# First gate maxima of an mLSTM reach their rows by products with a selection matrix instead of a trip through DRAM

## The chip, the cores and the metric

The kernel runs on one core of a Trainium2 chip. The metric is the device time of one execution in microseconds (us); the median of three runs stands for a kernel. Traces come from one further, profiled execution, whose span runs from the first to the last instruction of the program.

## What is computed

An mLSTM over 4 sequences of 768 tokens (8 heads of 40), followed by two mixture blocks on its 3072 x 320 output. All inputs and outputs count as float32, the weights of the blocks are given as float64. Cut to what matters:

```python
m_new = np.maximum(f_gate[:, :, t] + m, i_gate[:, :, t])       # running maximum of the gates
f_stab, i_stab = np.exp(f_gate[:, :, t] + m - m_new), np.exp(i_gate[:, :, t] - m_new)
C = f_stab * C + i_stab * (v k^T);  n = f_stab * n + i_stab * k
y[:, :, t] = sigmoid(o_gate) * (C q) / max(|n q|, 1)
...
h = (x @ w1) * (x @ w2) @ w3;  x = h @ w_out                    # first block
h = max(x @ w1, x @ w2, x @ w3);  out = h @ w_out               # second block
```

## The kernel before, in words

**Chunks.** Each sequence is cut into 9 chunks of 87 tokens (the last has 72), so there are 36 chunks, number q = 9 b + c. In a chunk the recurrence becomes matrix products: scores k.q, weighted by a decay matrix dd = exp(a_s - g_t) for key s and query t, where g is the running maximum of the gates (less the summed forget gates) and a is the gate value of each key. `prepare` (L786) loads a chunk's q, k and v, `visit` (L821) issues its score products (L839) and the products with v (L848), and `decay` (L744) makes dd.

**The gates** (L533 to L618) come by one DMA to 96 partitions: partition 32 i + 8 b + h holds chunks 3 i to 3 i + 2 of head h in sequence b. DVE scans them (L574, L585); the ends of the chunks are gathered to 32 partitions, scanned over the chunks, and spread again (L595, L607). L612 then leaves the running maxima in the tile gft, still on 96 partitions.

**The first nine decays** (q < 9, the chunks of sequence 0) are made by TensorE. A product (L757) of hl[0] (128 rows x 127 keys for each chunk) with hl[1] (128 rows x 8 heads x 88 queries) gives a_s - g_t for four heads at once, a second product (L758) adds -1e30 above the diagonal, and ScalarE takes the exponential (L761). To keep float32 precision with TensorE's faster operand type, every operand is split into a high part and the rest. Rows 0 to 63 of hl[0] hold the two parts of a, with unit rows of heads against them in hl[1]; rows 64 to 72 and 96 to 104 of hl[1] hold the two parts of g for the nine chunks, with -1 against them in hl[0]. So the maxima of sequence 0 have to get from partition 32 i + h, columns (c, t), to row 64 + 3 i + c, columns (h, t). Before the change that is a trip through DRAM: three writes to d_na (L619), one read back to the tile rv (L650), a ScalarE copy that makes the high part (L651) and a DVE subtraction that makes the rest (L652). GpSimd clears rows 64 to 127 of hl[1] first (L623). The other sequences write their maxima to d_na as well (L679), and the later decays read them from there; this part stays.

**Exponentials and sigmoids.** Five sigmoids of the first output gates (L667), on a tile loaded by L664, are made in one go, and every exponential of a decay is ordered behind all five (`after=sig`), since sigmoid and exponential use different tables of ScalarE.

**The folds.** The first block's w3 and w_out are multiplied on the chip (`fold`, L1227), eight times 16 product instructions of 320 columns (L1236); the result goes to wb (L1255, L1259). The weights come in granules of 128 x 512 float64 over the tiles sx and stg (`granule`, L1154): a DMA (L1167), a ScalarE step (L1172), a step that is made on DVE (L1181) or ScalarE (L1178), and a DVE step that joins the two (L1189). After the folds TensorE works through the two blocks, with the remaining chunks between their steps.

**The fill.** L541 issues 16 and then 6 products of zeros that warm up TensorE; the 6 wait for the first granule of w_out.

**What sets the order.** All this is written into a planner (`Plan`). Each operation has an engine (P TensorE, V DVE, A ScalarE, G GpSimd, D the DMA queue of SP), an estimated duration and the tiles that it reads and writes. A list scheduler takes, on each engine, the ready operation with the lowest entry in `PRIO`; where two engines can do an operation, `PICK` names one. The order that comes out is fixed in the program: every engine, and SP's DMA queue, works in that order and waits where an operation isn't ready. `WARM` tells the planner until when TensorE is slow.

```python
dma(150, lambda: SP.dma_start(out=raw_v, in_=d_na[0, :, :, 0:L]), r=[("dna", 0)], w=[("rv", 0)])   # L650
```

Of the kernel before, what the change touches and what calls it, by code (L numbers as in the profile page):

```python
# [65 lines left out]
    "11100111101000000100000110110011111101101111000111010011000110011110110011001110001111001011111110110000110010"  # L66
    "00001011101000111101100110011001101110001010010110011101001010110010111001101100101001110001001000001011111011"
    "10100110000001001110000011011110000100011011010111000100110110100000010000000000100100101000010100111101100110"
    "01000100010000101100001100010011010100110011110001011100000110011001110010111000000"
)  # L70
PRIO = (
# [95 lines left out]
)  # L167
WARM = 11500
USTEPS = (
# [1297 lines left out]
```

## Time and profile before

| | |
|---|---|
| median of three runs | 662.11 us (662.08 to 662.46) |
| the profiled execution: all of it | 664.29 us |
| the profiled execution: span | 662.6 us |
| mean granted TensorE clock | 0.997 |
| TensorE products busy | 648.7 us |
| DVE / ScalarE / GpSimd busy | 343.7 / 296.1 / 216.2 us |
| DMA | 76.12 MB, 115 GB/s on average |

The profiled execution is 2.18 us longer than the median. PE is TensorE's products, PEld its weight loads (which overlap products), ACT ScalarE, POOL GpSimd, SPq the DMA queue of SP. "Granted clock" is the share of full speed that TensorE was given.

### The profile page before, as it was taken

The numbers are of one execution on the slowest core, as the hardware profiler recorded it, in microseconds if no ns is written. First come the engines' busy times: TensorE is split into PE (matmuls) and PEld (weight loads), VectorE is DVE, ScalarE is ACT, GpSimd is POOL, SyncE is SP. The second block draws the span as 40 slices with busy tenths as digits, with TensorE's granted clock in tenths as the row PEclk, the third lists the DMA queues.
The fourth block names the chain that finished last, engine by engine and source line by source line (L and its number), as shares of the span: only waits on it lengthen the run. The fifth ranks groups of instructions, "written<-read, shape, count | busy, mean of one in ns | idle before, by whom it ended". The sixth has DMA issues, their size and how long they took to land.

```text
span 662.6 us, 14153 instructions
## 1 busy us (share of the span) xinstructions
PE 648.7 (98%) x5903; PEld 574.8 (87%) x5903; DVE 343.7 (52%) x623; ACT 296.1 (45%) x578; POOL 216.2 (33%) x235
## 2 busy tenths in 40 slices
PE   6899999999999999999999999999999999999997
PEld 5676899899999999999999988788788888888897
DVE  5688998877943663554543445464632321322222
ACT  7867986676622363453432343553331122322031
POOL 4052454566413234343244433562300013010030
PEclk9899999999999999999999999999999999999999
DMA  8989973545421453423122343342000010000011
GB/s 288 384 324 368 317 221 125 195 155 171 138 86 56 129 165 124 128 87 95 58 75 85 108 145 119 109 149 65 1 1 1 0 41 1 0 1 0 1 41 40
DMA packets 25489, 76.12 MB, mean 115 GB/s; under 512 B 3145, under 2 KB 6217, under 8 KB 25426
## 3 DMA queue, kind: packets, MB, share of 16 engines
q1 hardware_dynamic: 25426, 75.23, 33.8%
q8 instruction: 46, 0.75, 0.5%
q14 instruction: 17, 0.14, 0.1%
HBM read 71.18 MB, written 4.03 MB: 114 GB/s over the span
## 4 chain that ended last, share of the span: by engine, by line
PE 89%; DMA 3%; DVE 3%; ACT 3%; issue 1%; SPq 0%; ACTq 0%; DVEq 0%
PE wk L970 14%; PE wk L971 13%; PE wk L972 13%; PE wk L973 7%; PE acs L1102 6%; PE wk L975 5%; PE wk L1236 4%; PE aq L848 3%; PE acs L1082 3%; PE acs L1084 3%; PE acs L1086 3%; PE aq L839 3%; PE ac L1102 3%; PE ac L1082 2%; PE ac L1086 2%; PE wk L985 2%
## 5 line engine op out<-in xcount | busy, mean ns | idle before, releaser
L1049 DVE TENSOR_TENSOR misc<-misc,wk 128x384 f32<-128x384 f32 (+2 forms) x87 | 51.3, 594 | 130.5 <-PE wk L975 96.7
L997 ACT CAST hp<-misc 128x384 fp32r<-128x384 f32 (+2 forms) x101 | 55.0, 547 | 141.0 <-DVE misc L1049 53.1
L1001 POOL TENSOR_TENSOR hp<-misc,hp 128x384 fp32r<-128x384 f32 (+1 forms) x40 | 46.2, 1155 | 118.2 <-ACT hp L997 109.0
L970 PE MATMUL wk<-xx,wch 128*128 128x384 f32 (+1 forms) x216 | 77.3, 358 | 0.4 <-DVE misc L1049 0.4
L971 PE MATMUL wk<-xx,wcl 128*128 128x384 f32 (+1 forms) x216 | 76.5, 354 | 0.0
L972 PE MATMUL wk<-xx,wch 128*128 128x384 f32 (+1 forms) x216 | 76.5, 354 | 0.0
L1019 DVE TENSOR_TENSOR misc<-misc,wk 128x384 f32<-128x384 f32 (+1 forms) x56 | 33.8, 607 | 77.7 <-ACT misc L1017 53.2
L970 PE MATMUL wk<-xx,wah 128*128 128x384 f32 (+1 forms) x192 | 69.7, 363 | 1.1 <-DVE misc L1019 0.8
L971 PE MATMUL wk<-xx,wal 128*128 128x384 f32 (+1 forms) x192 | 68.1, 354 | 0.0
L972 PE MATMUL wk<-xx,wah 128*128 128x384 f32 (+1 forms) x192 | 68.0, 354 | 0.0
L1017 ACT COPY misc<-wk 128x384 f32<-128x384 f32 (+1 forms) x56 | 29.3, 522 | 54.8 <-PE wk L975 27.5
L1102 PE MATMUL acs<-wd,hp 128*128 128x320 f32 x234 | 52.7, 310 | 0.1
L1001 POOL TENSOR_TENSOR xx<-misc,hp 128x512 fp32r<-128x512 f32 (+1 forms) x15 | 18.2, 1215 | 95.5 <-ACT hp L997 91.3
L1046 ACT COPY misc<-wk 128x384 f32<-128x384 f32 (+1 forms) x42 | 22.1, 526 | 60.7 <-PE wk L975 46.2
L970 PEld LDWEIGHTS wk<-xx,wch 128*128 128x128 f32 x216 | 40.6, 188 | 3.7 <-DVE misc L1049 0.7
L972 PEld LDWEIGHTS wk<-xx,wch 128*128 128x128 f32 x216 | 40.5, 188 | 3.0
L971 PEld LDWEIGHTS wk<-xx,wcl 128*128 128x128 f32 x216 | 40.6, 188 | 2.8
L1236 PE MATMUL wk<-wof,w 128*128 128x320 f32 x128 | 38.4, 452 | 3.8 <-DVE wof L1189 2.3
L1102 PEld LDWEIGHTS acs<-wd,hp 128*128 128x128 f32 x234 | 40.0, 188 | 1.4 <-ACT misc L1145 0.3
L970 PEld LDWEIGHTS wk<-xx,wah 128*128 128x128 f32 x192 | 36.1, 188 | 4.6 <-DVE misc L1019 1.1
L972 PEld LDWEIGHTS wk<-xx,wah 128*128 128x128 f32 x192 | 36.1, 188 | 2.7
L973 PE MATMUL wk<-xx,wcr 128*128 128x384 f32 (+1 forms) x108 | 38.2, 354 | 0.0
(206 smaller groups left out, 1525.6 us busy)
## 6 DMA issues: line engine op xcount, KB each, us to landing
kv<-in_kv SPq DMA_DIRECT2D x32, 672.0 KB, 4.3
raw<-in_qk SPq DMA_DIRECT2D x36, 348.0 KB, 4.0
dd<-d_na SPq DMA_DIRECT2D x24, 348.0 KB, 3.8
sx<-in_w3t SPq DMA_DIRECT2D x9, 512.0 KB, 6.5
stg<-in_wc SPq DMA_DIRECT2D x9, 512.0 KB, 3.6
out<-misc SPq DMA_DIRECT2D x24, 160.0 KB, 1.9
stg<-in_w3t SPq DMA_DIRECT2D x6, 512.0 KB, 8.6
sx<-in_wa SPq DMA_DIRECT2D x6, 512.0 KB, 8.4
```

The source lines that it names most:

```text
L970: PE.matmul(p, lhsT=h_[:, kt], rhs=xh[:, kt], start=kt == 0, stop=False)
L971: PE.matmul(p, lhsT=l_[:, kt], rhs=xh[:, kt], start=False, stop=False)
L972: PE.matmul(p, lhsT=h_[:, kt], rhs=xl[:, kt], start=False, stop=False)
L973: PE.matmul(p, lhsT=r_, rhs=xh[:, 2], start=False, stop=False)
L975: PE.matmul(p, lhsT=r_, rhs=xl[:, 2], start=False, stop=True)
L997: P.op("A", act(n), lambda sl=sl: A.copy(out=T("ph", key)[:, sl], in_=T(*src)[:, sl]), r=[src + part], w=[("ph", key) + part])
L1001: e.tensor_tensor(out=T("pl", key)[:, sl], in0=T(*src)[:, sl], in1=T("ph", key)[:, sl].bitcast(F32), op=ALU.subtract)
L1019: P.op("V", dve(n), lambda: V.tensor_tensor(out=T(*sa), in0=T(*sa), in1=T(*ps[1]), op=ALU.mult), r=[ps[1]], w=[sa])
L1049: P.op("V", dve(sl.stop - sl.start), lambda sl=sl: V.tensor_tensor(out=T(*sc)[:, sl], in0=T(*sc)[:, sl], in1=T(*ps)[:, sl], op=ALU.max), r ...
L1082: PE.matmul(a, lhsT=w[:, o:o + 128], rhs=h_, start=st, stop=False)
L1102: PE.matmul(T(f"ac{m}", (k, 1)), lhsT=src[:, m * 128:m * 128 + 128], rhs=w[:, o:o + DM], start=first_, stop=last_,)
L1236: PE.matmul(T(*ps), lhsT=T(*w3)[:, i * 128:i * 128 + 128], rhs=wof[:, gt * 320:gt * 320 + 320], start=gt == 0, stop=gt == 7,)
```

## The change

The three writes, the read and the two splitting steps behind them are gone. Instead ScalarE makes the high part of gft and DVE the rest, both on 96 partitions, in a new tile gh (it lies in hp, as does sel). GpSimd builds a selection matrix sel (96 x 908, zeros but for a 1 in column 104 + i + 108 p of row 32 i + p). For each of the 8 heads, 6 products (two parts, three chunks of a partition) with a window of 112 columns of sel as weights and 88 columns of gh as moving operand add up to a PSUM tile rp in which every row is in place: rows 64 + 4 c + i for the high part, 96 + 4 c + i for the rest. ScalarE copies rows 64 to 111 of rp to hl[1], half the heads at a time. GpSimd clears rows 96 to 127 of hl[1] only; the pattern of -1 in hl[0] follows the new rows. The second part of the fill waits for gate values in the place of the first granule, and is ordered ahead of the new products. The planner's estimate for the load of the output gates goes from 1700 to 2050, WARM from 11500 to 8000, and all of PRIO and PICK is new.

```diff
 PICK = (
-    "1110011110100000010000011011001111110110111100011101001100011001111011001100111000111100101111111011000011
...
+    "0111010000100011100001011010100010110001111000010101111111000111100010110111110101000110111110110011110001
...
 PRIO = (
-    124, 456, 180, 57, 15, 275, 188, 113, 62, 171, 725, 164, 105, 490, 354, 463, 153, 364, 281, 60, 125, 68, 247, 137,
...
+    46, 26, 359, 120, 369, 213, 136, 142, 66, 141, 9, 8, 244, 134, 148, 319, 70, 72, 54, 28, 57, 50, 122, 37, 7, 2,
...
-WARM = 11500
+WARM = 8000
...
-    made["rv", 0] = misc[:, o:o + 8 * L]
...
+    made["gh", 0], made["sel", 0] = (hp[0:96, o:o + n].bitcast(F32R) for o, n in ((0, 2 * 3 * LE), (2 * 3 * LE, 908)))
+    made["gh", 0] = made["gh", 0].rearrange("p (x c t) -> p x c t", x=2, t=LE)
+    over["ph"] = over["pl"] = [("gh", 0), ("sel", 0)]
...
-    for n, dep in ((16, ()), (6, (("wo", 0, 0),))):
+    for n, dep in ((16, ()), (6, (("g", "git"),))):
...
-        e = cs[:, L + 1:L + 1 + NCH]
+        e = cs[:, L + 1:L + 1 + NCH].rearrange("p (i c) -> p i c", c=3)
         for o in (64, 96):
-            pick(e, e, 1, -o, [[-1, NCH]], ALU.not_equal, -1.0)
+            pick(e, e, 1, -o, [[-1, 3], [-4, 3]], ALU.not_equal, -1.0)
...
+    def f():
+        sel = T("sel", 0)
+        G.memset(sel.bitcast(F32), 0.0)
+        G.memset(T("gh", 0)[:, :, :, L:LE].bitcast(F32), 0.0)
+        for i in range(3):
+            sl = sel[32 * i:32 * i + 32]
+            pick(sl, sl.bitcast(F32), -108, -104 - i, [[1, 908]], ALU.not_equal, 1.0)
+
+    P.op("G", 36, lambda: G.memset(T("hl", 1)[96:128].bitcast(F32), 0.0), w=[("hl", 1, 2), ("hl", 1, 3)])
+    P.op("G", 3300, f, w=[("sel", 0), ("gh", 0, 2)])
...
-    for i in range(3):
-        dma(100, lambda i=i: SP.dma_start(
-            out=d_na[0, 3 * i:3 * i + 3].rearrange("c h t -> h c t"), in_=c3(T("g", "gft"))[32 * i:32 * i + 8]
-        ), r=[("g", "gft")], w=[("dna", 0, i)])
-
-    P.op("G", 400, lambda: G.memset(T("hl", 1)[64:128].bitcast(F32), 0.0), w=[("hl", 1, 2), ("hl", 1, 3)])
+    P.op("A", act(SL), lambda: A.copy(out=T("gh", 0)[:, 0, :, 0:L], in_=c3(T("g", "gft"))), r=[("g", "gft")], w=[("gh", 0, 0)])
+    P.op("V", dve(SL), lambda: V.tensor_tensor(
+        out=T("gh", 0)[:, 1, :, 0:L], in0=c3(T("g", "gft")), in1=T("gh", 0)[:, 0, :, 0:L].bitcast(F32), op=ALU.subtract
+    ), r=[("g", "gft"), ("gh", 0, 0)], w=[("gh", 0, 1)], port=1)
+    warm(1)
+    new(("rp", 0), [128, 2, 512], F32, "aq")
+
+    def rp(h):
+        return T("rp", 0)[0:112, h // 4, h % 4 * LE:h % 4 * LE + LE]
+
+    for g in range(2):
+
+        def f(g=g):
+            for h in range(4 * g, 4 * g + 4):
+                for x in range(2):
+                    for c in range(3):
+                        a = 40 + 108 * h - 32 * x - 4 * c
+                        PE.matmul(rp(h), lhsT=T("sel", 0)[:, a:a + 112], rhs=T("gh", 0)[:, x, c],
+                                  start=(x, c) == (0, 0), stop=(x, c) == (1, 2))
+
+        P.op("P", 24 * mm(LE), f, cols=24 * LE, r=[("gh", 0), ("sel", 0)], w=[("rp", 0, g)])
...
-    hi, raw_v = T("hl", 1)[64:64 + NCH, :, 0:L], T("rv", 0)[64:64 + NCH].rearrange("p (a b) -> p a b", b=L)
-    dma(150, lambda: SP.dma_start(out=raw_v, in_=d_na[0, :, :, 0:L]), r=[("dna", 0)], w=[("rv", 0)])
-    P.op("A", act(8 * L), lambda: A.copy(out=hi, in_=raw_v), r=[("rv", 0)], w=[("hl", 1, 2)])
-    P.op("V", dve(8 * L), lambda: V.tensor_tensor(
-        out=T("hl", 1)[96:96 + NCH, :, 0:L], in0=raw_v, in1=hi.bitcast(F32), op=ALU.subtract
-    ), r=[("rv", 0), ("hl", 1, 2)], w=[("hl", 1, 3)])
+    for g in range(2):
+        P.op("A", act(4 * LE, True), lambda g=g: A.copy(
+            out=T("hl", 1)[64:112, 4 * g:4 * g + 4], in_=T("rp", 0)[64:112, g, 0:4 * LE].rearrange("p (h t) -> p h t", t=LE)
+        ), r=[("rp", 0, g)], w=[("hl", 1, 2 + g)])
...
-    dma(1700, lambda: SP.dma_start(out=sg0.rearrange("p c d -> p (c d)"), in_=og),
+    dma(2050, lambda: SP.dma_start(out=sg0.rearrange("p c d -> p (c d)"), in_=og),
...
-            warm(1)
```

## Rows read from the trace of the kernel before

**Rows 1.** The page: busy us, share of the span and instructions of each engine.

```profile
PE 648.7 (98%) x5903; PEld 574.8 (87%) x5903; DVE 343.7 (52%) x623; ACT 296.1 (45%) x578; POOL 216.2 (33%) x235
```

**Rows 2.** Stretches: PE, PEld, DVE, ACT, POOL busy; granted clock, DMA share, GB/s.

```profile
12.00:14.00 2.00, 1.70 (x8) 1.20 (x8) 1.97 (x4) 1.33 (x2) 1.90 (x3) 1.00 1.01 272
14.00:16.00 2.00, 0.98 (x4) 0.38 (x2) 0.51 (x2) 1.33 (x3) 0.67 (x1) 1.00 0.86 286
16.00:18.00 2.00, 0.75 (x2) 0.62 (x3) 1.95 (x4) 2.00 (x4) 0.00 (x0) 0.91 0.99 365
18.00:20.00 2.00, 2.00 (x5) 1.27 (x4) 1.34 (x4) 0.82 (x2) 0.00 (x0) 0.50 0.98 397
```

**Rows 3.** Timeline of PE, 9.6 to 22 us: start, length, work [idle before].

```profile
11.11 1.15 PE L659 MATMUL ac<-cs,misc 32*127 32x32 f32 x9 [1.29 <-ACT sx L1172]
12.56 2.42 PE L1236 MATMUL wk<-wof,w 128*128 128x320 f32 x8 [0.30 <-DVE w L1189]
17.25 4.92 PE L1236 MATMUL wk<-wof,w 128*128 128x320 f32 x11 [2.27 <-DVE wof L1189]
```

**Rows 4.** The chain that ended last, whole span: start, length, link.

```profile
17.25 4.12 PE wk L1236 x8
...
33.57 2.15 PE wk L1236 x8
```

**Rows 5.** Timelines of ACT, 20 to 30 us, and of PE, 26.9 to 28.8 us.

```profile
23.99 0.77 ACT L651 CAST hl<-misc 9x696 fp32r<-9x696 f32 x1
...
26.02 0.83 ACT L667 ACTIVATE sg<-sg 96x320 f32<-96x320 f32 x2
...
28.17 0.46 ACT L761 ACTIVATE dd<-wk 87x348 f32<-87x348 f32 x1
...
28.67 0.54 PE L1236 MATMUL wk<-wof,w 128*128 128x320 f32 x1 [1.05 <-ACT dd L761]
```

**Rows 6.** SP's queue: timeline, 8 to 30 us; waits (us in all, times, longest).

```profile
17.86 0.30 SPq L650 DMA_DIRECT2D misc<-d_na  x1
...
SPq L650 <- DMA d_na<-misc: 2.8, 2, 2.6
```

**Rows 7.** Timeline of DVE, 11 to 18 us: the maxima.

```profile
11.14 0.43 DVE L612 TENSOR_TENSOR misc<-misc,mp 96x261 f32<-96x261 f32 x1
```

**Rows 8.** Groups of PEld, 0 to 30 us; then PE's timeline around 26 us.

```profile
L659 PEld LDWEIGHTS ac<-cs,misc 32*127 32x127 f32 x9 | 1.1, 185 | 1.7 <-POOL mp L595 1.7
...
25.59 0.85 PE L839 MATMUL aq<-raw 40*87 40x87 f32 x16
...
26.97 0.33 PE L758 MATMUL wk<-one 87*128 87x352 f32 x1
27.14 0.32 PE L757 MATMUL wk<-hl,hl 128*128 128x352 f32 x1
```

**Rows 9.** PE's waits after 60 us; the chain between 54 and 68 us.

```profile
PE wk L757 <- ACT dd L761: 1.1, 1, 1.1
PE wk L970 <- DVE misc L1019: 0.8, 1, 0.8
...
PE wk L757 <- ACT misc L1017: 0.2, 1, 0.2
...
55.74 7.37 DMA stg<-in_wa
```

**Rows 10.** POOL: a group by form, and its timeline before 8 us.

```profile
L780 POOL TENSOR_SCALAR_AFFINE_SELECT dd<-dd 87x696 f32<-87x696 f32 x24 | 21.4, 890 | 27.4 <-ACT dd L777 27.3
...
7.62 0.32 POOL L579 MEMSET misc<- 96x261 f32 x1 [4.17 <-DVE misc L574]
```

**Rows 11.** Timelines of DVE and POOL between 32 and 37 us.

```profile
32.93 0.68 DVE L1189 SCALAR_TENSOR_TENSOR w<-sx 128x512 int32<-128x512 int32 x1
...
34.67 1.82 DVE L1189 SCALAR_TENSOR_TENSOR w<-sx 128x512 int32<-128x512 int32 x1 [0.38 <-ACT sx L1178]
...
34.29 1.66 POOL L806 TENSOR_TENSOR pk<-kv,dd 63x696 f32<-63x696 f32 x1
```

More of the change, by code (lines that the diff above doesn't have):

```diff
@@ L65 @@
 PICK = (
[L66 to L69, printed above, removed]
+    "01110100001000111000010110101000101100011110000101011111110001111000101101111101010001101111101100111100011000"
+    "10010101001010000100101101101110111111010100101001111000100101101101000100110010111100000100000011010011111111"
+    "11111110101101100100010011110010100101111001101110101101000101010101011100101011100111001101010110101001110000"
+    "00100000110110110010100000011100101100111100000001001001101011000111011001110000000"
 )
 PRIO = (
[95 rows of a table removed]
[94 rows of a table added]
 )
-WARM = 11500
+WARM = 8000
 USTEPS = (
@@ L524, in mlstm_moe_kernel @@
         o += n
-    made["rv", 0] = misc[:, o:o + 8 * L]
-    for tag, (x, y) in where.items():
-        if x < o + 8 * L and o < y:
-            over[tag].append(("rv", 0))
+    made["gh", 0], made["sel", 0] = (hp[0:96, o:o + n].bitcast(F32R) for o, n in ((0, 2 * 3 * LE), (2 * 3 * LE, 908)))
+    made["gh", 0] = made["gh", 0].rearrange("p (x c t) -> p x c t", x=2, t=LE)
+    over["ph"] = over["pl"] = [("gh", 0), ("sel", 0)]
     def c3(t):
```

187 rows, old and new, of the table PRIO are left out of this document.

## Prediction

> **What bounds the kernel now.** I began with the page's table of engines: TensorE is busy for 648.7 of the 662.6 us of the span, every other engine for little more than half of it [rows 1]. So a change pays only where it shortens one of the few stretches in which TensorE does nothing useful, and it costs time where it gives TensorE work that doesn't fit into such a stretch. The changed code lies in the first 28 us, so I read those next, in steps of 2 us: between 12 and 18 us TensorE's share falls, and from 18 to 20 us its granted clock is 0.50, which is the 1.2 GHz level; the DMA engines stay near 1.0 there, apart from 14 to 16 us [rows 2]. The timeline of TensorE names the holes: it is idle for 1.29 us before the transposes at 11.11, for 0.30 before the first half of fold 0 at 12.56, and for 2.27 before the second half at 17.25 [rows 3]. That last hole ends with w_out granules which DVE finishes late; the trip through DRAM has no part in it. The second half, 8 instructions, then takes 4.12 us at the low clock, where 8 such instructions later take 2.15 [rows 4]: 1.97 us are lost to the clock, after a stretch of little TensorE work.
>
> Where does the trip itself end? Its last copy into hl[1] runs at 23.99 (DVE's subtraction follows), and the five sigmoids of the first output gates run around it until 26.85. The code lets no exponential of a decay start before all five, and another table of ScalarE has to be loaded first. The first exponential runs at 28.17, and TensorE idles 1.05 us for it [rows 5]. So the trip is mostly hidden behind the sigmoids; only its copy, 0.77 us, stands in ScalarE's order ahead of them. On SP's queue the trip costs more: three writes, then the read back, issued at 17.86 after a wait of 2.6 us for a write to land [rows 6].
>
> **The change, part by part.** My sum is made against the profiled execution (664.29 us in all, span 662.6); the median of the three plain runs, 662.11, is 2.18 lower, and I carry the difference over to it.
>
> *The products.* 48 products enter TensorE, each with a load of 112 columns of weights over 96 partitions and 88 moving columns; they can start when both parts of the maxima stand, about 12.6 us (the maxima are ready at 11.57 [rows 7], then a ScalarE and a DVE step of some 0.43 us each). No row shows such a product. The nearest is the nine transposes: loads of 127 columns that follow each other every (1.1 - 0.19)/8 = 0.114 us [rows 8], which for 112 columns is 0.10 us, or 4.8 us for 48. The lower end is the score products, 16 in 0.85 us: 0.053 each, 2.5 us. The upper end is the decay products of 352 columns, one every 0.16 us [rows 8]: 7.8 us, in case a product of few columns is charged like a long one. I take 4.8, since the transposes are the row with loads of nearly this size.
>
> One page speaks against the change here. The Trainium skill, "TensorE: Matmul & The Clock Gate", Part 3, "The mechanism", says that a weight load overlaps a running product only if it goes to other row groups, and all 48 use the same rows. The transposes also share their rows, and their loads ran on beneath the products, one every 0.114 us with a product of its own in each, so the trace doesn't bear the rule out.
>
> *What the products cover.* At 12.6 us they fill the hole of 2.27 us, and with TensorE at work there the clock should stay at its high level (2.4 GHz), which gives back 1.97. Together -4.2, against +4.8: +0.6 us for fold 0's end. The new ranks put the product groups (entries 24 and 25 of the list, counted from 0: 7 and 2) ahead of all of fold 0, so what is queued behind them is fold 0, and behind that everything on TensorE. If the clock stays low nevertheless, add 2.0.
>
> *ScalarE and the wait at 28.67.* The copy of 0.77 us and DVE's subtraction behind it leave this stretch. Added are a ScalarE copy and a DVE subtraction of 96 x 261 near 12 us and two evacuations of 352 columns (0.46 each, like the exponentials [rows 5]) near 18 us; in 14 to 20 us both engines have gaps [rows 2], so these cost nothing unless fold 0's granules come to stand behind them, at most 1.8 us. Of the wait of 1.05 us I take off 0.6: the sigmoids, and the gate values they load, still stand ahead. Bounds 0 and -1.05.
>
> *SP's queue and the DMA.* Four issues go, and the wait of 2.6 us, behind which loads of w3 for the folds were queued [rows 6]. But the DMA engines were 0.86 busy in 14 to 16 us and 0.99 after [rows 2], so they lose 0.14 x 2 = 0.3 us at least; by bytes, the 272 and 286 GB/s of 12 to 16 us against 365 just after, they lose (2 x 365 - 272 - 286)/365 x 2 = 0.9 us. That helps where TensorE waits for a load. The one such chain runs through w1's granule at 55.74 to 63.11 us and ends with a wait of 1.1 us [rows 9]. I take -0.6; bounds 0 and -0.9.
>
> *GpSimd.* It gets two clears and three selections of 32 x 908. From the selection of 696 columns, 0.89 us, each is 1.16; from the clear of 261, 0.32, the large clear is 1.11: 4.6 us, and a little for the small one. Its gap before 7.62 us is 4.17 [rows 10], and the clear of hl[1] shrinks to half its partitions. I cost it at nothing, covered by that gap; if the cover is short, the mask for the scan comes late, and with it the products.
>
> *The rest.* The transposes and their evacuation stay. Tile rp shares its place with the fill products, which end before the idle time of 1.29 us [rows 3], and with the first scores, which come at 25.59 [rows 8]: nothing. The fill's second part now waits for gate values instead of a granule; were it 1.29 us later, it would still end before the transposes can start: nothing. hp, in which the new operands lie, is first written when the first MoE block splits its products, long after the folds began: nothing.
>
> *The order.* All ranks and choices change, so any wait may move. After 60 us TensorE waits six times, for 1.1 us (the one above) and for 0.8, 0.5, 0.4, 0.3 and 0.2 [rows 9]: 2.2 us beside the first. I take 0 and allow 1.5 either way.
>
> Sum: 4.8 - 4.2 - 0.6 - 0.6 = **-0.6 us**: span 662.0, that execution 663.7, median **661.5**.
>
> **The rivals.** (a) *The products are cheap* and fit the hole with room to spare: at 0.053 us they take 2.5, so fold 0's second half starts when its granules stand and the sum is 2.3 lower, -2.9: 659.2. For it: the score products with 87 columns run at that rate. Against it: those use half the rows each, two at a time; these use 96. (b) *The products are dear*: 0.163 us each, 7.8 in all. Fold 0 ends 3.0 later than in my sum, and no idle time of that size stands between it and the end: +2.4, so 664.5, slower. It decides from about 0.14 us a product on (6.7 us, the sum then +1.3). For it: no product in the trace with this operand type has fewer than 320 columns. Against it: a load of 112 columns is the longer half of such a pair in the transposes. (c) *Loads and products take turns*: 0.10 + 0.163 x 88/352 = 0.14 us each, 6.8 us, sum +1.4: 663.5. That is the page's rule above; the transposes speak against it. (d) *GpSimd holds DVE*: a DVE step of two SBUF operands that takes 0.68 us took 1.82 while GpSimd worked [rows 11], and the selections now run while DVE turns the first granules and scans the gates, ahead of the maxima. One selection's length of delay, 1.16, on the gates and granules: sum +0.6, 662.7. The Trainium skill, "SBUF — State Buffer", "Who interferes with whom", describes this as a port pair that one of the two engines holds for a whole instruction; the 1.82 us agree. (e) *It doesn't matter*: the trip was hidden and the hole is given to other work; this lies inside my forecast's own range.
>
> **How the numbers follow.** About 0.2%, 1.3 us, is what a measurement can tell from no change. Chances: forecast 0.40, (a) 0.32, (b) 0.17, (c) 0.04, (d) 0.07. With its 1.5 us for the order and the bounds of the small terms, the forecast itself spans 660.0 to 663.0; of its 0.40 I put 0.06 faster than 660.8, 0.30 within 1.3 us of 662.1 and 0.04 above 663.4, where the order costs more than I allow. (a) is faster; (b) slower; (c) lies near the edge and is counted as slower; of (d) 0.06 is same and 0.01 slower. So faster 0.38, same 0.36, slower 0.26. The range runs from (a) less part (0.9) of the order's allowance, 658.3, to (b), 664.6.
>
> **What would show it.** Right: the 48 products every 0.10 us from about 12.6 us, no idle time before fold 0's second half, a granted clock near 1.0 from 16 to 22 us, fold 0 ended by 22 us, the first exponential some 0.8 us sooner, no SP wait near 17 us. Wrong: products spaced 0.14 us or more, the clock at 0.5 after them, or DVE steps before 8 us stretched beyond 1 us. If all that is right and the time still moves by over 1.5 us, the order did it: then TensorE's waits after 60 us differ from the list in [rows 9].

## The result, and the profile after

The changed kernel takes 669.47 us (667.89 to 669.79, 4 runs), the kernel before 662.29 on the same chip (662.08 to 662.84, 4 runs): 1.0102 times as long, 95% interval 1.0085 to 1.0120. It is slower by 7.2 us, and lies 4.9 above the upper end of the range. Its profiled execution took 669.34, with a span of 667.6 (5.0 above the one before) and a mean granted clock of 0.989.

The page's table of engines, beside [rows 1], and two rows of its 40 slices:

```profile
PE 657.3 (98%) x5951; PEld 583.4 (87%) x5951; DVE 341.4 (51%) x644; ACT 295.0 (44%) x577; POOL 193.5 (29%) x222
...
PE   7999999999999999999999999999999999999998
...
PEclk8799999999999999999999999999999999999999
```

TensorE has 48 more instructions and 8.6 us more busy time. The clock is down in the first two slices (17 us each) alone, so the loss is to be looked for there. TensorE's timeline of the changed kernel from the start (start, length, work, idle before it), beside [rows 3]:

```profile
1.67 6.88 PE L539 MATMUL aq<-wb 128*128 128x512 f32 x22 [1.67 <-DVE wb L533]
10.86 1.15 PE L681 MATMUL ac<-cs,misc 32*127 32x32 f32 x9 [2.32 <-DVE mp L604]
12.41 9.25 PE L644 MATMUL aq<-hp 96*112 96x88 f32 x48 [0.40 <-ACT hp L627]
21.45 4.42 PE L1257 MATMUL wk<-wof,w 128*128 128x320 f32 x8
25.40 0.63 PE L779 MATMUL wk<-hl,hl 128*128 128x352 f32 x1
25.87 0.33 PE L780 MATMUL wk<-one 87*128 87x352 f32 x1
26.03 2.32 PE L1257 MATMUL wk<-wof,w 128*128 128x320 f32 x8
```

From the first of the 48 products to the first of fold 0 (L1257) pass 21.45 - 12.41 = 9.04 us: 0.188 for each product, where I had 0.10. The holes ahead of fold 0's halves are gone, but fold 0 ends at 28.35 instead of 21.37. The stretches of the same execution, with the columns of [rows 2]:

```profile
10.00:12.00 2.00, 1.14 (x9) 1.07 (x9) 1.79 (x7) 1.20 (x2) 1.12 (x4) 0.97 1.03 418
12.00:14.00 2.00, 1.60 (x10) 1.61 (x9) 1.97 (x3) 1.95 (x4) 1.19 (x2) 0.50 1.04 423
14.00:16.00 2.00, 2.00 (x13) 2.00 (x13) 1.99 (x5) 0.00 (x0) 0.00 (x0) 0.50 0.99 397
16.00:18.00 2.00, 2.00 (x13) 2.00 (x12) 0.88 (x2) 0.00 (x0) 0.00 (x0) 0.50 1.01 321
...
24.00:26.00 2.00, 2.00 (x6) 1.33 (x6) 1.52 (x4) 1.97 (x3) 0.00 (x0) 0.62 0.03 8
26.00:28.00 2.00, 2.00 (x10) 1.36 (x8) 0.65 (x1) 1.31 (x3) 0.00 (x0) 1.00 0.83 264
```

The granted clock falls to 0.50 (1.2 GHz) just ahead of the first product, at about 11.9 us if the 0.97 of 10 to 12 us is one drop, and comes back only at about 25.5 (0.62 of 24 to 26), at the end of fold 0's first half. Weight loads (the second number) fill the whole of the stretches from 14 to 18 us. Two more things stand out: ScalarE has nothing to do between 14 and 20 us, and between 24 and 26 us the DMA engines rest. ScalarE's timeline (beside [rows 5]) and SP's queue (beside [rows 6]) say why:

```profile
21.75 0.45 ACT L674 CAST hl<-aq 48x352 fp32r<-48x352 f32 x1 [7.80 <-PE aq L644]
22.21 0.67 ACT L1194 ACTIVATE sx<-sx 128x512 f32<-128x512 f32 x1
...
31.78 0.46 ACT L783 ACTIVATE dd<-wk 87x348 f32<-87x348 f32 x1
```

```profile
17.79 7.90 SPq L1189 DMA_DIRECT2D stg<-in_w3t  x2
```

ScalarE's copy out of rp waits 7.80 us for the products, with granule steps (L1194) queued behind it, and SP's queue takes 7.90 us over two loads, 7.4 of them a wait for a DVE step (L1203) behind those. Which of these two, TensorE's own time or this blockade, makes the loss, the trace alone doesn't tell; the experiments do.

GpSimd's timeline, DVE's with a step that needs its mask, and the first two of TensorE's waits after 60 us, beside [rows 10] and [rows 9] (the DVE rows begin with the first scan of the gates):

```profile
2.82 2.91 POOL L546 TENSOR_SCALAR_AFFINE_SELECT hp<-hp 32x908 fp32r<-32x908 f32 x3
...
7.86 0.32 POOL L588 MEMSET misc<- 96x261 f32 x1
```

```profile
5.77 0.70 DVE L583 TENSOR_TENSOR_SCAN misc<-misc 96x261 f32<-96x261 f32 x1 [3.75 <-DMA misc<-in_gi]
...
8.37 0.70 DVE L594 TENSOR_TENSOR_SCAN misc<-misc 96x261 f32<-96x261 f32 x1 [0.83 <-POOL misc L589]
...
11.06 0.43 DVE L621 TENSOR_TENSOR misc<-misc,mp 96x261 f32<-96x261 f32 x1
```

```profile
PE wk L992 <- ACT misc L1068: 0.8, 1, 0.8
PE wk L992 <- DVE misc L1071: 0.6, 1, 0.6
```

The three selections took 2.91, the maxima stand at 11.49 (11.57 before), and the 1.1 us wait for an exponential isn't in the list any more.

### The profile page after: what moved, and what is told of

Same layout as the page of the kernel before. It is cut to its first block, busy times and chain, and to the rows that moved or that the text cites. A ratio compares the mean times of both kernels' runs of the same rounds, so it can differ in the third digit from the quotient of the medians.

```text
span 667.6 us, 14270 instructions
## 1 busy us (share of the span) xinstructions
PE 657.3 (98%) x5951; PEld 583.4 (87%) x5951; DVE 341.4 (51%) x644; ACT 295.0 (44%) x577; POOL 193.5 (29%) x222
## 4 chain that ended last, share of the span: by engine, by line
PE 88%; ACT 3%; DVE 3%; DMA 2%; issue 1%; POOL 1%; POOLq 0%; DVEq 0%; ACTq 0%
PE wk L992 13%; PE wk L993 13%; PE wk L994 13%; PE wk L995 6%; PE acs L1124 6%; PE wk L1257 5%; PE wk L997 5%; PE aq L870 3%; PE aq L861 3%; PE acs L1104 3%; PE ac L1124 3%; PE acs L1106 3%; PE acs L1108 3%; PE wk L1007 1%; PE wk L946 1%
## 5 line engine op out<-in xcount | busy, mean ns | idle before, releaser
L1023 POOL TENSOR_TENSOR hp<-misc,hp 128x384 fp32r<-128x384 f32 (+1 forms) x44 | 52.0, 1182 | 127.5 <-ACT hp L1019 116.5
L1257 PE MATMUL wk<-wof,w 128*128 128x320 f32 x128 | 38.9, 454 | 0.0
L895 DVE TENSOR_TENSOR pk<-aq,dd 87x696 f32<-87x696 f32 (+1 forms) x33 | 28.4, 862 | 19.3 <-PE aq L870 18.4
```

Source lines behind the costliest of these rows:

```text
L1023: e.tensor_tensor(out=T("pl", key)[:, sl], in0=T(*src)[:, sl], in1=T("ph", key)[:, sl].bitcast(F32), op=ALU.subtract)
L1257: PE.matmul(T(*ps), lhsT=T(*w3)[:, i * 128:i * 128 + 128], rhs=wof[:, gt * 320:gt * 320 + 320], start=gt == 0, stop=gt == 7,)
```

## The experiments

The theory (A): the products are paced by their weight loads, 112 columns each, and the load's pace follows the granted clock; the clock falls around 12 us, the products neither hold nor raise it, and so 48 of them take 9 us instead of 4.8. Its rivals: a fixed price for each product, or loads and products in turns (B); the blockade of ScalarE and SP's queue (D); the new order of everything else (C). "Before" is 663.05 us (661.01 to 665.39, 14 runs) beside the first four kernels, 663.04 (660.32 to 664.94, 23 runs) beside the next four, and 662.44 (660.11 to 666.2, 17 runs) beside the last three.

### e1_narrow: only the 48 columns that are read

Rows 0 to 63 of rp are zeros that nobody reads. Here the window of sel is 48 columns wide, and the result lies in rows 0 to 47.

```diff
-        return T("rp", 0)[0:112, h // 4, h % 4 * LE:h % 4 * LE + LE]
+        return T("rp", 0)[0:48, h // 4, h % 4 * LE:h % 4 * LE + LE]
...
-                        PE.matmul(rp(h), lhsT=T("sel", 0)[:, a:a + 112], rhs=T("gh", 0)[:, x, c],
+                        PE.matmul(rp(h), lhsT=T("sel", 0)[:, a + 64:a + 112], rhs=T("gh", 0)[:, x, c],
...
-            out=T("hl", 1)[64:112, 4 * g:4 * g + 4], in_=T("rp", 0)[64:112, g, 0:4 * LE].rearrange("p (h t) -> p h t", t=LE)
+            out=T("hl", 1)[64:112, 4 * g:4 * g + 4], in_=T("rp", 0)[0:48, g, 0:4 * LE].rearrange("p (h t) -> p h t", t=LE)
```

> Edit of the changed kernel: the products load 48 columns of sel (those of the rows that are used) in place of 112, and rp holds the rows at 0 to 47; what is computed and the order stay the same. Theory A (the products are paced by their weight loads, 0.187 us for 112 columns at the granted clock of 0.50): a product every 48/112 x 0.187 = 0.080 us, or 3.9 us for 48 where they took 9.25, so ScalarE, which waited 7.80 us for them, goes on 5.4 us sooner; the time falls by 3 to 5.4 us from 669.5, to 664.1 to 666.5. Rival B (a product of 88 columns costs 0.187 us whatever it loads): the pace and the 9.25 us stay, 669.5. Rival C (the new order later in the program costs the time, the products don't): the products may be faster, but the time stays within 1 us of 669.5.

Measured: 662.62 us (660.29 to 664.03, 10 runs), ratio to before 0.9992 (0.9973 to 1.0010). TensorE's timeline, then two of its stretches:

```profile
13.06 3.83 PE L644 MATMUL aq<-hp 96*48 96x88 f32 x45 [0.18 <-DVE hp L628]
16.68 3.60 PE L1257 MATMUL wk<-wof,w 128*128 128x320 f32 x8
...
20.45 2.32 PE L1257 MATMUL wk<-wof,w 128*128 128x320 f32 x8
```

```profile
14.00:16.00 2.00, 2.00 (x29) 2.00 (x28) 1.99 (x5) 0.02 (x1) 0.00 (x0) 0.50 0.98 393
...
18.00:20.00 2.00, 2.00 (x8) 1.37 (x6) 1.15 (x3) 1.93 (x5) 0.00 (x0) 0.72 0.86 262
```

45 products take 16.68 - 13.06 = 3.62 us, 0.080 each, at a clock of 0.50. The moving columns, the rows and the count are those of the changed kernel, and 0.188/0.080 = 2.35 is the ratio of the loads' columns, 112/48 = 2.33. So the 88 moving columns add nothing beside a load of 112. The whole loss goes with it, more than I had expected, since the clock is also back by 20 us instead of 26. B and C fall.

### e2_longfill: the clock held up to the products

```diff
-        def f(n=n):
+        def f(n=n + 8 * (n == 6)):
```

Eight more products of zeros in the fill's second part.

> Edit of the changed kernel: the second part of the fill has 14 products of zeros where it had 6, so that TensorE has dense work to about 10.3 us, where it fell idle at 8.5; the order stays the same. Theory A1 (the clock fell at 11.9 us because TensorE was idle from 8.5 to 10.9, and products then run at the clock they find): granted clock 1.0 from 12 to 26 us, the products every 0.094 to 0.10 us, 4.7 us in all, fold 0's products at 0.27 us each; the time falls by 5.5 to 7, to 662.5 to 664. Theory A2 (the products with their short moving side can't keep the clock up): the clock falls a few us later than 11.9, within the products or behind them, the time falls by 1 to 4. Rival B (the cost of a product doesn't come from the clock): products at 0.187 us, time 669.5 or more.

Measured: 668.22 us (667.09 to 670.05, 5 runs), ratio 1.0068 (1.0043 to 1.0092). The transposes ahead of the products:

```profile
11.10 1.15 PE L681 MATMUL ac<-cs,misc 32*127 32x32 f32 x9 [0.61 <-DVE mp L604]
```

The products' line in two stretches, 13.3 to 15.3 us and 16 to 19 us (form, count: shortest/median/longest in ns, first and last start), and the clock from 14 us on:

```profile
L644 PEld LDWEIGHTS aq<-hp x22: 173/178/178, 13.3 to 15.3; 96*112 96x112 f32 x22
...
L644 PEld LDWEIGHTS aq<-hp x18: 307/307/307, 15.8 to 18.9; 96*112 96x112 f32 x18
```

```profile
14.00:16.00 2.00, 2.00 (x21) 2.00 (x21) 1.99 (x4) 0.21 (x1) 0.00 (x0) 0.91 0.99 399
16.00:18.00 2.00, 2.00 (x13) 2.00 (x12) 1.12 (x3) 0.00 (x0) 0.00 (x0) 0.50 0.84 293
```

One kernel, one stream of products, both prices: at the high clock 22 loads start within 2.0 us, 0.10 apart, which is the value I had taken; then the clock falls in the middle of the products, though TensorE never pauses, and 18 loads need 3.1 us, 0.18 apart. So here the products did not hold the clock, as theory A2 has it. The estimate of a product was right for 2.4 GHz; the assumption of 2.4 GHz was not.

### e3_zeros_between: more work among the products

```diff
                                   start=(x, c) == (0, 0), stop=(x, c) == (1, 2))
+                PE.matmul(acs[:, 512 * x:512 * x + 512], lhsT=wb[:, NA - 1, 512:640], rhs=wb[:, NA - 1, 0:512], start=True, stop=True)
```

After each six products, one of 512 columns of zeros.

> Edit of the changed kernel: one product of zeros with 512 columns behind each six of the new products, eight in all, into a PSUM tile that is not yet in use; nothing else. Work added: 8 x 0.43 = 3.4 us at the low clock, 8 x 0.22 = 1.8 at the high one. Theory A (the low clock is what the products cost): either the denser work lifts the clock within the products, then they and the fold behind them run at the high clock sooner and the time falls by 1 to 4 us in spite of the work added; or it doesn't, then the clock stays at 0.50 to 26 us or later, and the time rises by up to 3.4, to 673. Rival B: the clock may rise, but the products stay at 0.187 us and the time rises by 1.8 or more.

Measured: 672.13 us (671.64 to 675.04, 4 runs), ratio 1.0137 (1.0097 to 1.0177). Two of its stretches:

```profile
20.00:22.00 2.00, 2.00 (x10) 1.88 (x10) 0.00 (x0) 0.00 (x0) 0.00 (x0) 0.50 1.00 387
...
26.00:28.00 2.00, 2.00 (x5) 1.22 (x4) 1.06 (x3) 1.93 (x5) 0.00 (x0) 0.50 0.00 0
```

The clock stayed at 0.50 until 28 us, and the median is 2.7 us above the 669.47 of the changed kernel, within the 3.4 allowed. More work of this kind between the products didn't lift the clock here. Since the clock never rose, this run doesn't tell A from B; e1 and e2 do.

### e4_before_again: the kernel before, profiled once more

> The kernel before, once more, for its granted clock: the profiled execution shown had a stretch at 0.50 from 17.4 to 21.4 us and took 664.29 us, the plain runs 662.1. If that stretch comes and goes from execution to execution, a profile without it spans about 660.5 us and takes 662.2; if it belongs to the kernel, it is there again, at the same place, with 664.3 us.

Measured: 660.28 us, one execution, mean clock 1.000. Its timeline around fold 0, and the stretch that had a clock of 0.50 in [rows 2]:

```profile
12.04 2.42 PE L1236 MATMUL wk<-wof,w 128*128 128x320 f32 x8 [0.30 <-DVE w L1189]
15.39 6.73 PE L1236 MATMUL wk<-wof,w 128*128 128x320 f32 x24 [0.93 <-DVE wof L1189]
```

```profile
18.00:20.00 2.00, 2.00 (x9) 1.44 (x8) 1.38 (x4) 1.98 (x3) 0.00 (x0) 1.00 1.03 403
```

Here the kernel before has no stretch at the low clock, and its hole is 0.93 us, not 2.27. So much of the 4.2 us that the products were to cover wasn't there in this execution. Of the 54 executions of the kernel before beside the experiments 16 have a mean clock of 0.999 or 1.000, so the low stretch is short or missing in those too; how long their holes were is not on record.

### e5_narrow_longfill: both together

The edits of e1_narrow and e2_longfill in one kernel.

> Edit of the changed kernel: both edits of before, 48 columns of weights and 14 products of zeros in the second part of the fill. The clock held to 15.6 us with the longer fill, and a product with 112 columns then came every 0.0985 us. Theory A (a product is paced by its load): 48/112 x 0.0985 = 0.042 us each, 2.0 in all, where the narrow products alone took 3.8 at the low clock. A1: with the products over by 15 us the clock doesn't fall, fold 0 runs at 0.27 us a product: 3.5 us less than the 662.6 of the narrow products alone, 659. A2: it falls behind the products all the same, and fold 0 runs at half the rate: 1.8 less, 660.8. Rival B (a floor of some 0.08 us for each product, whatever its load): 662.

Measured: 662.10 us (660.05 to 666.88, 12 runs), ratio 0.9991 (0.9973 to 1.0009): no gain over e1_narrow that can be told. That is the number of rival B, a floor of 0.08 for each product; the trace doesn't decide it, for its clock was low during most of the products, but e11 does (below). The profiled execution, the slowest of the twelve, has this stretch:

```profile
12.00:14.00 2.00, 1.28 (x15) 1.10 (x15) 1.97 (x3) 2.00 (x5) 1.27 (x2) 0.75 1.04 424
```

Here the clock fell at the beginning of the products, in spite of the longer fill. In five of the twelve executions the mean clock was 1.000, in none of the 22 of e1 and e9 over 0.997; but those five took 660.05 to 663.84 too. So the longer fill carries the clock through at times, and with narrow products that is then worth little.

### e6_copies_dont_wait: the blockade without its cause

```diff
-            out=T("hl", 1)[64:112, 4 * g:4 * g + 4], in_=T("rp", 0)[64:112, g, 0:4 * LE].rearrange("p (h t) -> p h t", t=LE)
+            out=T("hl", 1)[64:112, 4 * g:4 * g + 4], in_=wb[0:48, NA - 2, 0:4 * LE].bitcast(F32).rearrange("p (h t) -> p h t", t=LE)
```

ScalarE's two copies read a constant, in a tile that DVE sets early, so the kernel leaves out that the maxima reach the decays; the 48 products still run.

> Edit of the changed kernel: the two copies into hl[1] read a tile with a constant (set early by DVE), not rp. This leaves out that the maxima reach the decays; the 48 products of 112 columns still run, but nothing reads them. Theory A (TensorE's own time is what counts): ScalarE no longer waits 7.80 us, the granules are turned sooner, but the products still take 9.25 us at the low clock and fold 0 starts at 21.5 us: the time falls by less than 1.5 from that of the changed kernel beside it. Rival D (ScalarE, blocked behind the products, starves the folds and SP's queue, and that is the greater part): the time falls by 3 or more.

Measured: 669.65 us (669.51 to 670.99, 4 runs), ratio 1.0105 (1.0079 to 1.0131), beside 668.88 for the changed kernel in the same group (e8). TensorE, and one stretch:

```profile
12.31 9.25 PE L644 MATMUL aq<-hp 96*112 96x88 f32 x48 [0.22 <-ACT hp L627]
21.35 4.32 PE L1257 MATMUL wk<-wof,w 128*128 128x320 f32 x8
```

```profile
24.00:26.00 2.00, 2.00 (x7) 1.37 (x6) 0.00 (x0) 0.00 (x0) 0.00 (x0) 0.69 1.02 389
```

The DMA engines are busy between 24 and 26 us now (1.02 instead of 0.03), and ScalarE has nothing left to do in that stretch; the time doesn't fall. D falls: the blockade, the most striking thing in the trace, cost nothing here.

### e7_no_products: the rest of the change alone

```diff
-                        PE.matmul(rp(h), lhsT=T("sel", 0)[:, a:a + 112], rhs=T("gh", 0)[:, x, c],
-                                  start=(x, c) == (0, 0), stop=(x, c) == (1, 2))
+                        pass
```

and the copies as in e6.

> Edit of the changed kernel: as the one whose copies read a constant, and the 48 products left out, so that the maxima don't reach the decays; order and all else stay the same. Theory A (the products are the loss): fold 0 starts near 12.5 us and the time falls by 8 to 10.5 from that of the changed kernel beside it, to 659 to 661.5, below the kernel before. Rival C (the new order and the other new steps cost time too): it stays above 663.

Measured: 663.78 us (663.09 to 664.63, 10 runs), ratio 1.0013 (0.9997 to 1.0029). TensorE's timeline:

```profile
15.13 4.55 PE L1257 MATMUL wk<-wof,w 128*128 128x320 f32 x8 [3.29 <-DVE w L1211]
...
19.84 2.32 PE L1257 MATMUL wk<-wof,w 128*128 128x320 f32 x8
```

The products cost 669.65 - 663.78 = 5.9 us against e6, from which this kernel differs by them alone (5.1 against e8); the rest of the change, order and all, 0.7 against the kernel before, which this run can't tell from nothing. I had expected more to come back, and by the bound that I gave (above 663) the run went rival C's way, though it lies level with the kernel before. The reason is that without the products fold 0 waits 3.29 us for a granule that DVE joins at 14.65 (behind its subtraction for hl[0]), and then starts at the low clock: the products do cover a hole, and the new order has made it longer than the 2.27 and 0.30 of [rows 3] together.

### e8_changed_again: the changed kernel beside e5 to e7

> The changed kernel once more, on the chip of the other runs of this group, as their base. 669.5 within 1 us; granted clock 0.50 from about 12 to 26 us again, products every 0.187 us. If its clock falls later in this execution, the products before the fall come every 0.0985 us, as in the run with the longer fill.

Measured: 668.88 us (668.47 to 670.06, 4 runs), ratio 1.0092 (1.0066 to 1.0118). The 45 products behind the first three took 8.42 us, 0.187 each, as before. The clock fell somewhat later here, among the first products (0.70 on average from 12 to 14 us).

### e9 to e11: can the rest be won by order?

e9 is e1_narrow again. e10 gives DVE's subtraction for hl[0] a later rank, so that fold 0's granule is joined first; e11 also ranks the second 24 products behind fold 0's first half.

```diff
-    206, 1, 33, 124, 103, 153, 196, 239, 117, 52, 203, 335, 41, 186, 536, 74, 422, 283, 464, 738, 133, 349, 221, 334,
+    206, 1, 33, 900, 103, 153, 196, 239, 117, 52, 203, 335, 41, 186, 536, 74, 422, 283, 464, 738, 133, 349, 221, 334,
```

```diff
-    46, 26, 359, 120, 369, 213, 136, 142, 66, 141, 9, 8, 244, 134, 148, 319, 70, 72, 54, 28, 57, 50, 122, 37, 7, 2,
+    46, 26, 359, 120, 369, 213, 136, 142, 66, 141, 9, 8, 244, 134, 148, 319, 70, 72, 54, 28, 57, 50, 122, 37, 40, 41,
```

> The narrow products of e1_narrow once more, as the kernel that the two next to it are compared with. Theory (loads set the products' pace, the granted clock sets the load's): products every 0.080 us at the low clock, 0.042 to 0.045 at the high one; time within 0.2% of the kernel before, 661.5 to 664 where that stands at 663. Rival (e1's gain came from its chip or its executions): 666 us or more.

> Narrow products, and DVE's step for hl[0] (1.44 us) ranked behind the steps of fold 0's granules. Theory (what is left of the loss stands in fold 0's granules, which DVE makes late): DVE's granule step at L1211 runs about 1.4 us earlier, the first half of fold 0 starts at 16.7 us or before, as the products let it, with no wait in front of it; but the products end at about 16.9 us already in e1_narrow, with the second half's granules as the next thing waited for, so the gain is at most 1 us: 661 to 663. Rival (the products alone set fold 0's start): fold 0's halves as in e9_narrow_again, time the same within 0.2%. Rival (any new order costs or gives a few us): a time outside 660 to 665.

> As e10, and the second 24 narrow products ranked behind fold 0's first half, so that they stand in the hole ahead of its second half. Theory: the first half of fold 0 starts about 1.9 us earlier (24 x 0.080), near 14.9 us or when its granules stand, the later 24 products fill the hole ahead of the second half, and fold 0 ends about as much earlier as the hole was long (0.17 us in e1_narrow), so next to nothing: 661 to 663. If dense fold products raise the clock sooner when they come sooner, the clock is back before 19.5 us and 1 us more is won: 660 to 662. Rival (what is written on ScalarE for the later half then delays the first decays): the wait for the first exponential grows past 1.5 us and the time is 663 to 665.

Measured: e9 662.95 us (660.37 to 663.99, 12 runs), ratio 0.9998 (0.9982 to 1.0014); e10 674.92 (674.33 to 678.16, 6 runs), ratio 1.0191 (1.0166 to 1.0216); e11 676.03 (674.14 to 677.30, 5 runs), ratio 1.0198 (1.0175 to 1.0221). In e10 the edit did what it was for (DVE's timeline, then TensorE's):

```profile
13.25 0.52 DVE L1211 SCALAR_TENSOR_TENSOR w<-stg 128x256 int32<-128x256 int32 x1
```

```profile
16.63 3.20 PE L1257 MATMUL wk<-wof,w 128*128 128x320 f32 x8
...
19.99 2.32 PE L1257 MATMUL wk<-wof,w 128*128 128x320 f32 x8
```

The granule is joined 1.6 us sooner (14.83 in the changed kernel), and fold 0 ends at 22.31, no later than in e1_narrow (22.77). The 12 us are lost elsewhere: one changed rank made the list scheduler arrange the whole kernel anew. TensorE's waits after 60 us in e10, the first four:

```profile
PE wk L992 <- ACT misc L1039: 2.0, 3, 0.9
PE wk L946 <- DVE misc L933: 1.9, 1, 1.9
PE wk L992 <- ACT dd L783: 1.8, 2, 1.1
PE wk L992 <- ACT misc L1068: 1.2, 1, 1.2
```

All such waits sum to 8.9 us there and 2.2 in e9; that is 6.7 of the 11.1 between the two spans (673.2 and 662.1). What the other 4.4 are was not followed up. So e10 and e11 say nothing of their own question: it stays open whether the narrow products can be placed better. They do say what "ranks anew" may cost: 12 us, where I had allowed 1.5. No version here is faster than the kernel before; e1_narrow and e5 are level with it.

One thing e11 does show, for its first 24 products ran before the clock fell (TensorE's timeline, then the stretch):

```profile
13.02 1.17 PE L644 MATMUL aq<-hp 96*48 96x88 f32 x21 [0.32 <-DVE hp L628]
14.00 1.40 PE L1257 MATMUL wk<-wof,w 128*128 128x320 f32 x2
...
12.00:14.00 2.00, 1.29 (x25) 1.20 (x25) 2.00 (x5) 1.97 (x4) 1.29 (x2) 1.00 1.04 424
```

At a granted clock of 1.00 the narrow products come every (14.00 - 13.02)/21 = 0.047 us. So the 0.080 of e1 is no fixed floor, and rival B of e5 falls. Whether it is still the load that paces a product of 48 weight columns isn't shown: 88 moving columns at the rate of the decay products (352 in 0.163 us, [rows 8]) take 0.041, and twice that at half the clock, so both sides would give nearly the same.

## Why the prediction was wrong

The step that failed is in the part on what the products cover: "with TensorE at work there the clock should stay at its high level (2.4 GHz), which gives back 1.97". The clock fell just ahead of the products or among their first in the changed kernel and in e1, e3 and e5, and in the midst of their unbroken stream in e2. It rose again only once fold 0's products ran, never during the 48 (e7, which has none of the 48, also had it low, from its idle stretch until fold 0 ran). What the products met instead of a high clock was 0.188 us each. A second step hangs on it: "If the clock stays low nevertheless, add 2.0" priced the low clock for fold 0 alone and left the products at 0.10 us. They double too, so that even the upper bound of 7.8 us, taken from rows at the high clock, was too low.

A term put at nothing bears on the first step: the fill. The prediction asked only whether its second part might end too late. It ended earlier, at 8.55 us where the trace before has 9.82 (its last product, below), and TensorE stood idle for 2.32 us ahead of the transposes instead of 1.29. With the longer fill of e2 the idle time is 0.61, and the clock fell at about 15.6 us (0.91 of 14 to 16) instead of 11.9; in the kernel before it fell at about 17.6 (0.91 of 16 to 18, [rows 2]). So in these executions the change also brought the fall forward, ahead of the products. A longer fill alone, as in e2, gives little back: 1.0068 for 1.0102, with intervals that overlap. What makes the clock fall where it does stays open.

```profile
9.43 0.39 PE L541 MATMUL aq<-wb 128*128 128x512 f32 x1
```

The same sum with measured terms, against the profiled execution before (span 662.6):

| term | predicted | measured, and where |
|---|---|---|
| 48 products | +4.8 | +9.04 (12.41 to 21.45) |
| hole of 2.27 covered | -2.27 | -2.27 (gone) |
| clock in fold 0's halves | -1.97 | -0.27 (first half 3.95 for 2.42, second 2.32 for 4.12) |
| products start | 0 | -0.15 (12.41 for fold 0's 12.56) |
| wait for the first exponential | -0.6 | -1.05 (gone) |
| SP's queue, DMA, and the order: waits after 60 us | -0.6 | -0.9 (2.4 in six waits for 3.3; the one of 1.1 is gone) |
| sum | -0.6 | +4.4 |

The span grew by 5.0; these rows leave 0.6 of it open. (Two decay products, 0.63 us, now run between fold 0's halves instead of later; they are left out of the sum.) Of fold 0, one half runs at the low clock before and after, only not the same one, so next to nothing came back there. Four kernels, each by its own profiled execution (fold 0's end is start plus length of its second half in the timelines above):

| kernel | each product, us | fold 0 ends | time of that execution | difference |
|---|---|---|---|---|
| e7_no_products | none | 22.16 | 663.81 | 641.7 |
| e1_narrow | 0.080 | 22.77 | 662.16 | 639.4 |
| e2_longfill | 0.10, then 0.18 | 25.88 | 667.09 | 641.2 |
| changed | 0.188 | 28.35 | 669.34 | 641.0 |

Fold 0's end moves by 6.2 us through this list, and what follows it by 2.3 without any trend: the loss is made ahead of fold 0's end. (By the same reckoning e3, e6, e8 and e9 have 640.2 to 641.4, and e5, in the longest of its twelve executions, 643.7.) The median moved by 7.2 us, more than the 5.0 between the two profiled executions, because the one before was itself 2.18 above its median; e4 shows a cause for such a difference, a low stretch that some executions have and others don't. That e4's hole was 0.93 says the same of the cover: the products had less to hide behind than [rows 3] showed.

**By points.** *Right:* the products' start; 0.10 us a product at the high clock; that TensorE would not wait ahead of fold 0's second half; the first exponential no longer waited for (in e1 too, where it runs at 26.19 for 28.17). *Right by luck:* that GpSimd's selections cost nothing (2.91 us for three where I had 3.5). The cover was in fact short: DVE waits 0.83 us for the mask behind them, which it didn't before; the gates' first scan ran at 5.77 instead of 6.81, and so the maxima came no later all the same. Also by luck: that the two evacuations on ScalarE are free. They blocked it for 7.80 us with granules behind them, which I had bounded by 1.8, and only e6 shows that this cost nothing, because TensorE was late itself. *Wrong:* the clock, hence the sign.

**The rivals.** (b), "dear products", has the right sign and nearly the right price (0.163 for 0.188) by a wrong cause: it charges a product like a long one at the high clock, where e2 has 0.10. (a) falls with the same row. (c), loads and products in turns, falls: it asks for 0.14 at the high clock, where e2 has 0.10, and at the low clock the pace falls in proportion to the loads' columns, which leaves nothing for the 88 moving ones (e1 against the changed kernel). The Trainium skill, "TensorE: Matmul & The Clock Gate", Part 3, "The mechanism", says in its list of what overlaps that a load overlaps running products only in other row groups, while its paragraph above that list also lets loads into a background weight buffer be pulled ahead. All these loads use the same 96 rows, so the measurement differs from the list. The Trainium skill, under the same title, section "LDWEIGHTS (loading the stationary operand)", gives the columns divided by 1.2 as the nanoseconds of a load, which makes an estimate of 93 for 112 columns. e2's 0.10 us agrees at 2.4 GHz, while at 1.2 GHz the runs show twice that (0.187). (d) is not seen: while the selections ran (2.82 to 5.73 us), DVE was waiting for the load of the gates, until 5.77, so there was nothing to hold. (e) held for the rest of the change (e7), not for the products.

What I could have read in the profile: [rows 2] and [rows 4] show that the clock falls after 16 us and that a fold half then takes 1.9 times as long. The nearest row for the products, the transposes, was read at the high clock only; doubling it gives 0.20 us each, 9.6 in all, and a forecast of about 668 for the case "the clock is low there". That case deserved a place among the rivals, with the products repriced and not fold 0 alone.

## What to carry to other kernels

A price for a TensorE instruction belongs to a clock level: where work is put into a stretch beside a drop of the granted clock, work out the sum at both levels, and don't count on small products with wide weight loads to keep the clock (in e2 it fell among them). Where a product's moving side is shorter than its weight side, as 88 against 112 here, the weight columns set its pace, so load only the columns whose results are read: 48 instead of 112 took back the whole loss here. And where a scheduler derives the order from ranks, a single rank can move more than the change under study; undo the change's parts with the order held fixed.

## What the runs showed of the hardware that was not expected

- Products of 88 columns with loads of 112 run at the pace of the loads: 0.10 us at a granted clock of 1.00 and 0.187 at 0.50; with loads of 48 columns 0.047 at 1.00 (e11) and 0.080 at 0.50. Per weight column at 0.50 that is 1.67 ns in both cases.
- TensorE busy for 2.00 of 2.00 us doesn't mean that the clock is high: in e3 it was so from 14 to 28 us at a granted clock of 0.50.
- The low stretch comes and goes between executions of one kernel. Those of the kernel before have mean clocks of 0.991 to 1.000 and times from 660.1 to 666.2; of the changed one, 0.989 to 0.992 in all eight.
